# When the sums of a group of heads leave PSUM, and where the last group's sums lie: sigmoid attention before two gated MLPs

## Chip, core and metric

The kernel runs on one core of a Trainium2 chip. The metric is the device time of one execution in microseconds (us), as a median over runs; lower is better. The engines are named as the profile names them: PE multiplies matrices (PEld are its weight loads), ACT computes activations and copies, DVE does elementwise work and 32x32 transposes, SP issues nearly all DMAs. PE writes its results to PSUM, eight banks of 2 KB per partition, and ACT or DVE bring them from there to SBUF.

## What is computed

```python
# q, k, v: (4, 12, 448, 64), float32
scores = scale * np.matmul(q, k.transpose(0, 1, 3, 2)) - np.log(S)
attn = 1.0 / (1.0 + np.exp(-scores))
attn_out = np.matmul(attn, v)                 # 4 batches, 12 heads
x = attn_out.transpose(0, 2, 1, 3).reshape(4, 448, 768)
# then two gated MLPs in a row, each: h = act(x @ w_in); u, v = halves of h
# v normalized over its columns, then mixed over the sequence by w_spatial, plus b_spatial
# out = (u * mixed v) @ w_out        (the second adds its own x)
```

The attention is a sigmoid, not a softmax, so no row of scores has to be complete before its values can be summed.

## The kernel before

The attention works on groups of four heads, numbered n = 0 to 11 (three per batch, batches in the order 1, 0, 3, 2). The 448 keys are cut in chunks r = 0, 1, 2 of 128 keys and a rest r = 3 of 64. `scores` computes one chunk for the four heads of a group (24 matmuls, L500, each head in its own 32 rows of the array), `scores_rest` the rests of an even group and of the odd one behind it together (L518). Such a step is called a unit here; `weigh` puts two sigmoids on ACT behind it (L473, one per two heads, tiles a and ar).

`values` sums attention times v. An item (r, x) is the chunk r for the two heads of the pair x; a group has eight, and all go to one tile av of two banks: x = 0 in its first bank, x = 1 in its second. An item is two fp32 matmuls (L538), and the profile shows each of these as two records, so that four records are one item. When all four items of a pair are summed, `gather` copies the pair's bank to SBUF on ACT (L558): two copies (392 and 70 columns) in an odd batch, one of 448 in an even one.

Two consecutive groups, an even and an odd one, take 7 units, and 42 units in all are laid out in a fixed order. `units` and `sums` say which items follow which unit. PE and ACT run this order as it is written; nothing reorders it. The even group's last items are (3,0), (2,0), (2,1), all behind one unit, (3,0) bringing both pairs. The odd group's are (1,1), (2,0) behind one unit and (0,1), (2,1) behind the next; that next unit is the L518 one.

PSUM in the attention is four tiles of two banks, in a ring: a unit of scores takes two tiles from its head and gives them back once its sigmoids are issued, a group takes one for av with its first item and gives it back once it is gathered. So a unit, or a group's first item, waits until ACT has read what its tile held before. These waits are set by the framework from the tiles' uses; they are for a whole tile: an item that writes the second bank of av waits for a copy issued earlier out of the first.

Behind the last unit `done` puts six casts of the first MLP's input on ACT (L659) and six subtractions on DVE (L660). The last group's last four items come behind it in the program, then the first MLP, which opens with `hv` (L672, 18 matmuls of 512 columns into a tile t of the pool ps_t). The PSUM pools of the MLPs (ps_t, ps_av, ps_sc) are laid where the attention's pool ps_att was, and ps_t's first tile waits for what was in that pool at its place.

The lines that matter: L350 the ring, L352 `banks_of`, L526 to L548 `values` with `gather`'s calls, L558 the copies, L608 the warm-up that takes the ring's last tile, L933 and L943 to L945 the pools.

Of the kernel before, what the change touches and what calls it, by code (L numbers as in the profile page):

```python
# [9 lines left out]
F32 = mybir.dt.float32  # L10
# [16 lines left out]
def tile_sigmoid_attention_two_gated_mlps(  # L27
# [36 lines left out]
    P = 128  # L64
# [17 lines left out]
    xs = [const.tile([P, KF * ROW + PAD], F32, name=f"x{i}") for i in range(B // 2)]  # L82
# [256 lines left out]
    spatial.waiting = [load_w_sp(l1, j) for j in range(4)]  # L339


    def attention(apool, epool, ps_att, done):
        G = H // 4
        NG = B * G

# [1 line left out]
            b, i = divmod(n, G)  # L347
            return b ^ 1, i

        ring, open_sums = list(range(4)), {}  # L350

        def banks_of(k, name):  # L352
            return ps_att.tile([P, 2, 512], F32, tag=f"s{k}", name=name, bufs=1)
        raws, turned, ops, vs, att = {}, {}, {}, {}, {}

        def load_qk(n, xs="kq"):
# [109 lines left out]
        def score_banks():  # L466
            ks = [ring.pop(0) for _ in range(2)]
            return ks, [banks_of(k, "sc") for k in ks]
# [57 lines left out]
        def values(n, r, x):  # L526
            if n not in open_sums:
                k = ring.pop(0)
                open_sums[n] = k, banks_of(k, "av"), [0, 0]
            k, av, count = open_sums[n]  # L530
            vt, vr = vs[n]
            xs = (x,) if r < 3 else (0, 1)
            for x in xs:
                at = REST * ((x + n) % 2)
                ps = slice(at, at + REST)
                for o in range(2):
                    h = 2 * x + o
                    nc.tensor.matmul(  # L538
                        av[o * D:(o + 1) * D, x, :S],
                        vt[:, h, r] if r < 3 else vr[ps, o], att[n, r][:, h] if r < 3 else att[n, r][ps, h],  # L540
                        start=(count[x] == 0), stop=(count[x] == 3),
                    )
                count[x] += 1
            for x in xs:
                if count[x] == 4:
                    gather(n, x, av[:, x])
            if count == [4, 4]:
                ring.append(k)  # L548

        def gather(n, x, av):  # L550

            b, i = place(n)
            y = chunk_of(b, 2 * i + x)
            o = av[:, :S].rearrange("p (c t) -> p t c", c=TC)

            def back(at, t0, t1):
                dst = y[:, at:at + (t1 - t0) * TC]
                nc.scalar.copy(out=dst.rearrange("p (t c) -> p t c", c=TC), in_=o[:, t0:t1])  # L558

            if b % 2 == 0:  # L560
                back(0, 0, 32)
            else:
                t = 3 * P // TC
                back(SPAN, 0, t + 1)
                back(S - 3 * P % TC, t, 32)
# [34 lines left out]
        def weigh_up(s):  # L600
            for n, r, x in sums.get(s, ()):
                values(n, r, x)
# [3 lines left out]
        load_qk(1, "qk")  # L606
        later.pop("rows")()
        warm = banks_of(ring[-1], "av")[:, 0]  # L608
        for _ in range(9):
            nc.tensor.matmul(warm[:, :P], ident, ident, start=True, stop=True)  # L610
        turn(0)
        for s in range(U + 2):
# [3 lines left out]
            n = 2 * p + (1 if step < 2 else 2 if step < 6 else 3)  # L616
# [10 lines left out]
            if step in (0, 4):  # L627
                n = 2 * p + 2 + step // 4
# [8 lines left out]
            if s >= U:  # L637
                spatial.tick(1)

        return open_sums[NG - 1][0]  # L640


    class Mlp:
# [279 lines left out]
    with tc.manual_schedule():  # L923
# [4 lines left out]
        apool = tc.tile_pool(name="apool", bufs=1)  # L928
# [1 line left out]
        m1, m2 = Mlp(l1), Mlp(l2)  # L930

        psum = bass.MemoryType.PSUM
        ps_att = tc.tile_pool(name="ps_att", bufs=1, space=psum)  # L933

        def operands_made():
            apool.__exit__(None, None, None)
# [3 lines left out]
            m1.split_x(0, 0, KD)  # L940

        with tc.tile_pool(name="epool", bufs=1, side="right") as epool:
            last = attention(apool.__enter__(), epool, ps_att.__enter__(), operands_made)  # L943
        ps_att.__exit__(None, None, None)
        for x in ("ps_av", "ps_t", "ps_sc") if last == 0 else ("ps_t", "ps_av", "ps_sc"):  # L945
            later[x] = ctx.enter_context(tc.tile_pool(name=x, bufs=2, space=psum))

        later["opool"] = ctx.enter_context(tc.tile_pool(name="opool", bufs=1))
        with tc.tile_pool(name="fpool", bufs=1) as fpool:
# [47 lines left out]
            for b in range(B):  # L997
                last = b == B - 1
# [56 lines left out]
            for b in range(B):  # L1055
                last = b == B - 1
# [85 lines left out]
```

## Time and profile before

| | us |
|---|---|
| median of 3 runs | 562.26 (561.35 to 564.97) |
| profiled execution | 561.34 |
| its span on the core | 559.6 |
| PE busy in the span | 547.8 (98%) |
| ACT busy | 217.5 (39%) |
| DVE busy | 359.6 (64%) |

The span runs from the first to the last instruction that the profile shows; 1.74 us of the profiled execution lie around it. The attention takes about the first 144 us, the two MLPs the rest. A busy PE is one on which a matmul is in flight.

### The profile page before, as it was taken

To read this page: it belongs to the slowest core of one execution; us is meant where nothing else is said; L and a number is where in the kernel's file an instruction comes from. 1 tells how busy PE (TensorE), PEld (TensorE's weight loads), DVE (VectorE), ACT (ScalarE), POOL (GpSimd) and SP (SyncE) were. 2 spreads that over 40 slices of the span, in tenths; PEclk is the share of its full clock that TensorE was granted. 3 is DMA by queue.
4 is the path that set the end of the run, shared out by engine and by line. 5 is a ranking of instruction groups with operands and counts; after the bars stand their busy time and mean duration, and the time that the engine had idled before them with its cause. 6 is when DMAs were issued, how large, how long until landed. Compare 5 with 4: busy or idle time off the path is not lost.

```text
span 559.6 us, 9090 instructions
## 1 busy us (share of the span) xinstructions
PE 547.8 (98%) x3486; PEld 438.6 (78%) x3486; DVE 359.6 (64%) x749; ACT 217.5 (39%) x373; POOL 32.5 (6%) x62
## 2 busy tenths in 40 slices
PE   8999999999899999999999999999999999999997
PEld 5445444454589899898898889998999889989886
DVE  6999897882388789899764987851542173324311
ACT  6676666677234142353352146320311042103101
POOL 0000000000020100200200012000100020001000
PEclk9999999999999999999999999999999999999999
DMA  8878646341232165363336443200410032003003
GB/s 280 223 220 257 188 138 229 102 146 48 47 96 70 62 177 126 86 179 104 113 125 163 116 131 117 85 0 1 77 24 0 2 57 43 1 11 60 15 1 112
DMA packets 95531, 56.44 MB, mean 101 GB/s; under 512 B 67328, under 2 KB 83712, under 8 KB 95488
## 3 DMA queue, kind: packets, MB, share of 16 engines
q1 hardware_dynamic: 95344, 55.60, 36.5%
q8 instruction: 27, 0.44, 0.4%
q10 hardware_dynamic: 144, 0.26, 0.1%
q14 instruction: 16, 0.13, 0.1%
HBM read 44.83 MB, written 11.01 MB: 100 GB/s over the span
## 4 chain that ended last, share of the span: by engine, by line
PE 94%; ACT 4%; DMA 1%; DVE 0%; issue 0%; ACTq 0%
PE t L672 17%; PE t L718 17%; PE av L538 10%; PE sc L804 10%; PE sc L500 8%; PE t L738 6%; PE av L804 5%; PE av L738 3%; PE sc L738 3%; PE sc L814 3%; PE t L900 3%; PE av L900 3%; ACT a L473 3%; PE sc L518 2%; PE av L814 1%; PE t L814 1%
## 5 line engine op out<-in xcount | busy, mean ns | idle before, releaser
L473 ACT ACTIVATE a<-sc,small 128x896 f32<-128x896 f32 x72 | 67.3, 1007 | 29.6 <-PE sc L500 29.1
L538 PE MATMUL av<-a,vt 128*64 128x448 f32 x288 | 62.3, 552 | 6.4 <-ACT xe L558 3.5
L681 DVE BATCH_NORM_STATS2 st<-vr 128x6 f32<-128x512 f32 x28 | 19.4, 694 | 70.2 <-ACT vr L678 70.2
L678 ACT ACTIVATE vr<-t 128x512 f32<-128x512 f32 x28 | 16.7, 598 | 95.4 <-PE t L672 95.4
L500 PEld LDWEIGHTS sc<-opq,opk 32*128 32x128 f32 x840 | 39.8, 183 | 17.9 <-issue 12.7
L538 PEld LDWEIGHTS av<-a,vt 128*64 128x64 f32 x288 | 17.4, 136 | 44.6 <-issue 27.8
L500 PE MATMUL sc<-opq,opk 32*128 32x448 f32 x840 | 49.9, 373 | 0.0
L672 PE MATMUL t<-vh,xh 128*128 128x512 f32 x112 | 41.6, 392 | 0.6 <-ACT xe L558 0.6
L748 DVE SCALAR_TENSOR_TENSOR gt<-t,bb 128x448 f32<-128x448 f32 x16 | 10.9, 682 | 45.7 <-PE t L738 45.7
L683 POOL TENSOR_SCALAR st<-st 128x1 f32<-128x1 f32 x28 | 10.8, 384 | 472.1 <-DVE st L682 472.1
L672 PE MATMUL t<-vh,xl 128*128 128x512 f32 x98 | 38.2, 390 | 0.0
L756 ACT CAST gh<-u 128x448 fp32r<-128x448 f32 (+1 forms) x16 | 8.6, 540 | 71.8 <-DVE u L752 71.8
L718 PE MATMUL t<-xh,uh 128*128 128x448 f32 x96 | 34.8, 363 | 0.0
L718 PE MATMUL t<-xh,ul 128*128 128x448 f32 x96 | 34.8, 362 | 0.0
L718 PE MATMUL t<-xl,uh 128*128 128x448 f32 x96 | 34.6, 360 | 0.0
L738 PE MATMUL t<-sh,v 128*128 128x448 f32 x112 | 32.8, 362 | 0.0
L672 PE MATMUL t<-vl,xh 128*128 128x512 f32 x84 | 32.7, 389 | 0.0
L660 DVE TENSOR_TENSOR xl<-x,xh 128x512 fp32r<-128x512 f32 (+1 forms) x32 | 20.0, 654 | 19.1 <-ACT xh L659 19.1
L718 PE MATMUL t<-xh,vl 128*128 128x448 f32 x96 | 29.6, 362 | 0.0
L723 ACT ACTIVATE u<-t 128x448 f32<-128x448 f32 x32 | 17.4, 544 | 24.9 <-PE t L718 24.7
L700 ACT CAST v<-vr 128x512 fp32r<-128x512 f32 x24 | 14.9, 621 | 30.5 <-DVE vr L692 30.5
L672 PE MATMUL t<-m,xh 128*128 128x512 f32 x84 | 26.4, 395 | 0.0
(210 smaller groups left out, 1280.3 us busy)
## 6 DMA issues: line engine op xcount, KB each, us to landing
w<-in_moe_w_in_dram SPq DMA_DIRECT2D x24, 256.0 KB, 3.2
inq<-in_q_dram SPq DMA_DIRECT2D x12, 448.0 KB, 5.7
ink<-in_k_dram SPq DMA_DIRECT2D x11, 448.0 KB, 5.1
vt<-in_v_dram SPq DMA_DIRECT2D x48, 96.0 KB, 3.7
w<-in_moe_w_out_dram SPq DMA_DIRECT2D x18, 256.0 KB, 3.0
we<-in_moe_w_in_dram SPq DMA_DIRECT2D x6, 512.0 KB, 4.4
we<-in_moe_w_in_dram SPq DMA_DIRECT2D x8, 384.0 KB, 3.8
out_dram<-y SPq DMA_DIRECT2D x48, 56.0 KB, 1.9
```

Of the source, the lines that this page charges most:

```text
L473: nc.scalar.activation(a[:, dst], sc[x][..., :S], AF.Sigmoid, bias=bias_s, scale=scale)
L500: nc.tensor.matmul(banks[h][:, :S], opk[ps, x, o:o + P], opq[ps, y, S * j:S * (j + 1)], start=(t == 0), stop=(t == 5), tile_position=(32 * ...
L538: nc.tensor.matmul(av[o * D:(o + 1) * D, x, :S], vt[:, h, r] if r < 3 else vr[ps, o], att[n, r][:, h] if r < 3 else att[n, r][ps, h], star ...
L660: nc.vector.tensor_tensor(out=pair[1][:, :n], in0=src, in1=raw(pair[0][:, :n]), op=ALU.subtract)
L672: nc.tensor.matmul(ps[:, :FF], a, w, start=(c == 0 and n == 0), stop=(c == self.kc - 1 and n == 2),)
L681: nc.vector.bn_stats(out=st, in_=vr)
L718: nc.tensor.matmul(ps[:, :S], w, a, start=(c == 0 and n == 0), stop=(c == self.kc - 1 and n == 2),)
L723: nc.scalar.activation(u, ps[:, :S], AF.Relu if L.n == 1 else AF.Gelu_apprx_tanh)
L738: nc.tensor.matmul(ps[:, :S], a, w, start=(n == 0), stop=(n == len(todo) - 1))
L804: nc.tensor.matmul(self.o[m][:, :n_cols], w, a, start=(not second and i == 0 and n == 0), stop=(second and i == KF - 1 and n == 2),)
L814: nc.tensor.matmul(ps[:, :cols.stop - cols.start], a, w, start=(not second and i == 0 and n == 0), stop=(second and i == KF - 1 and n == 2),)
L900: nc.tensor.matmul(ps[:, :FF], x, w[:, c], start=(c == 0 and n == 0), stop=(c == KD - 1 and n == 2),)
```

## The change

`gather` is called for both pairs when the whole group is summed (`count == [4, 4]`), not for each pair when its own four items are. The rest item of an odd group takes its pairs in the order 1, 0. So it reads partitions 0 to 63 first and 64 to 127 behind them, as an even group's does. The ring starts as [0, 3, 1, 2], and tile 3 comes from a pool of its own, ps_last. It is the same ring with its tiles renamed, so that the last group's av is tile 3. ps_last is closed first, then ps_att, and the three pools of the MLPs come in one fixed order, which is also the one that the program took before.

```diff
@@ attention
-        ring, open_sums = list(range(4)), {}
+        ring, open_sums = [0, 3, 1, 2], {}
 
         def banks_of(k, name):
-            return ps_att.tile([P, 2, 512], F32, tag=f"s{k}", name=name, bufs=1)
+            pool = ps_att if k < 3 else ps_last
+            return pool.tile([P, 2, 512], F32, tag=f"s{k}", name=name, bufs=1)
@@ values
-            xs = (x,) if r < 3 else (0, 1)
+            xs = (x,) if r < 3 else (n % 2, 1 - n % 2)
...
                 count[x] += 1
-            for x in xs:
-                if count[x] == 4:
+            if count == [4, 4]:
+                for x in range(2):
                     gather(n, x, av[:, x])
-            if count == [4, 4]:
                 ring.append(k)
@@ the pools
-        ps_att = tc.tile_pool(name="ps_att", bufs=1, space=psum)
+        ps_att, ps_last = [tc.tile_pool(name=x, bufs=1, space=psum) for x in ("ps_att", "ps_last")]
...
+        ps_last.__exit__(None, None, None)
         ps_att.__exit__(None, None, None)
-        for x in ("ps_av", "ps_t", "ps_sc") if last == 0 else ("ps_t", "ps_av", "ps_sc"):
+        for x in ("ps_t", "ps_av", "ps_sc"):
             later[x] = ctx.enter_context(tc.tile_pool(name=x, bufs=2, space=psum))
```

Lines from L354 to L543 stand one lower in the changed kernel (L538 is L539 there, L473 is L474, L500 is L501); L558 and what follows stand where they stood.

On ACT, around the end of the first odd group (n = 1), the order before: six sigmoids of three units, the copies of pair 0 (392 and 70 columns), the sigmoids of the L518 unit, the copies of pair 1.

```order
L473 ACTIVATE a<-sc,small 128x896 x6
L558 COPY x_65<-av 128x392
L558 COPY x_65<-av 128x70
L473 ACTIVATE ar<-sc,small 128x896 x2
L558 COPY x_65<-av 128x392
L558 COPY x_65<-av 128x70
L473 ACTIVATE a<-sc,small 128x896 x6
```

The same place now:

```order
L474 ACTIVATE a<-sc,small 128x896 x6
L474 ACTIVATE ar<-sc,small 128x896 x2
L558 COPY x_65<-av 128x392
L558 COPY x_65<-av 128x70
L558 COPY x_65<-av 128x392
L558 COPY x_65<-av 128x70
L474 ACTIVATE a<-sc,small 128x896 x6
```

Pair 0's copies have moved behind the sigmoids of one more unit. Around an even group's end ACT's order is as it was; there the copies' waits change.

On PE, the end of the last group (n = 11) and the first matmuls of the MLP, with the engines that each row waits for in brackets (names with DMAHW are loads that have landed). Before, the eight matmuls of the last items (1,1), (2,0), (0,1), (2,1) and `hv`:

```order
L538 MATMUL av<-a,vt 64x448 [waits Activation_49]
L538 MATMUL av<-a,vt 64x448
L538 MATMUL av<-a,vt 64x448 [waits Activation_49]
L538 MATMUL av<-a,vt 64x448
L538 MATMUL av<-a,vt 64x448 [waits Activation_49]
L538 MATMUL av<-a,vt 64x448 x3
L672 MATMUL t<-vh_73,xh 128x512 [waits DMAHW3_49,DMAHW2_49,DMAHW4_49,DMAHW1_49,DMAHW5_49,DMAHW0_49,DMAHW6_49,DVE_49,Activation_49]
```

and now:

```order
L539 MATMUL av<-a,vt 64x448 [waits Activation_49]
L539 MATMUL av<-a,vt 64x448
L539 MATMUL av<-a,vt 64x448 [waits Activation_49]
L539 MATMUL av<-a,vt 64x448 x3
L539 MATMUL av<-a,vt 64x448 [waits Activation_49]
L539 MATMUL av<-a,vt 64x448
L672 MATMUL t<-vh_73,xh 128x512 [waits DMAHW3_49,DMAHW2_49,DMAHW4_49,DMAHW1_49,DMAHW5_49,DMAHW0_49,DMAHW6_49,PE_49,Activation_49]
```

The fifth matmul, the first of item (0,1), no longer waits for ACT. The seventh now waits for the sigmoid of its own second pair of heads, which a wait on the later copy covered before. `hv` still waits for ACT, but for another instruction there: by the semaphore values of the two programs it was the second gather copy, and it is the first L659 cast now.

## Rows read from the trace of the kernel before

**Rows 1.** Stages: window and its us, then busy us of each engine (instructions), PE clock, DMA
```profile
5.53:144.53 139.00, 131.93 (x1448) 64.56 (x1449) 115.76 (x220) 94.81 (x129) 0.00 (x0) 1.00 0.60 179
144.53:540.00 395.47, 395.47 (x1927) 356.06 (x1928) 240.43 (x520) 118.45 (x237) 31.81 (x56) 1.00 0.29 73
```

**Rows 2.** Waits of PE: who waited for whom, us in total, times, longest
```profile
PE av L538 <- ACT xe L558: 3.5, 3, 2.0
PE av L538 <- ACT x L558: 2.8, 4, 0.7
```

**Rows 3.** Timeline of PE, groups 0 and 1: start, us, instructions, [idle before and releaser]
```profile
17.05 0.98 PE L538 MATMUL av<-ar,vr 64*64 64x448 f32 x8
17.97 0.97 PE L538 MATMUL av<-a,vt 128*64 128x448 f32 x4
19.64 0.97 PE L538 MATMUL av<-a,vt 128*64 128x448 f32 x4 [0.70 <-ACT x L558]
20.55 2.70 PE L500 MATMUL sc<-opq,opk 32*128 32x448 f32 x48
23.20 1.08 PE L538 MATMUL av<-ar,vr 64*64 64x448 f32 x8
24.21 1.72 PE L538 MATMUL av<-a,vt 128*64 128x448 f32 x8
25.86 1.50 PE L500 MATMUL sc<-opq,opk 32*128 32x448 f32 x24
...
30.64 1.72 PE L538 MATMUL av<-a,vt 128*64 128x448 f32 x8
32.29 2.74 PE L500 MATMUL sc<-opq,opk 32*128 32x448 f32 x48
```

**Rows 4.** Timeline of ACT in the same stretch
```profile
17.08 1.90 ACT L473 ACTIVATE a<-sc,small 128x896 f32<-128x896 f32 x2 [0.59 <-PE sc L500]
18.99 0.60 ACT L558 COPY x<-av 128x392 f32<-128x392 f32 x2
...
30.81 1.91 ACT L473 ACTIVATE ar<-sc,small 128x896 f32<-128x896 f32 x2 [0.95 <-PE sc L518]
32.60 0.60 ACT L558 COPY x<-av 128x392 f32<-128x392 f32 x2
33.89 3.71 ACT L473 ACTIVATE a<-sc,small 128x896 f32<-128x896 f32 x4 [0.68 <-PE sc L500]
```

**Rows 5.** Timeline of PE, groups 9 to 11 and the first MLP's start
```profile
122.60 2.74 PE L500 MATMUL sc<-opq,opk 32*128 32x448 f32 x48
...
130.76 0.97 PE L538 MATMUL av<-a,vt 128*64 128x448 f32 x4
132.40 0.97 PE L538 MATMUL av<-a,vt 128*64 128x448 f32 x4 [0.66 <-ACT x L558]
133.30 2.71 PE L500 MATMUL sc<-opq,opk 32*128 32x448 f32 x48
...
136.97 3.23 PE L538 MATMUL av<-a,vt 128*64 128x448 f32 x16
142.17 1.72 PE L538 MATMUL av<-a,vt 128*64 128x448 f32 x8 [1.98 <-ACT xe L558]
144.53 0.50 PE L672 MATMUL t<-vh,xh 128*128 128x512 f32 x1 [0.63 <-ACT xe L558]
```

**Rows 6.** Timeline of ACT in that stretch
```profile
122.88 0.54 ACT L558 COPY x<-av 128x448 f32<-128x448 f32 x1
...
138.47 2.19 ACT L659 CAST xh<-x 128x512 fp32r<-128x512 f32 x4
...
141.57 0.55 ACT L558 COPY xe<-av 128x448 f32<-128x448 f32 x1
```

**Rows 7.** Groups of the page: weight loads of the scores (busy us, mean ns | idle)
```profile
L500 PEld LDWEIGHTS sc<-opq,opk 32*128 32x128 f32 x840 | 39.8, 183 | 17.9 <-issue 12.7
```

**Rows 8.** Timeline of DVE: operands of group 2, subtractions for the first MLP
```profile
22.04 1.08 DVE L456 TENSOR_TENSOR opq<-tq,opq 128x896 fp32r<-128x896 f32 x1
...
139.13 2.50 DVE L660 TENSOR_TENSOR xl<-x,xh 128x512 fp32r<-128x512 f32 x4 [10.42 <-ACT xh L659]
```

More of the change, by code (lines that the diff above doesn't have):

```diff
@@ L339, in tile_sigmoid_attention_two_gated_mlps, with attention @@
     spatial.waiting = [load_w_sp(l1, j) for j in range(4)]
-    def attention(apool, epool, ps_att, done):
+    def attention(apool, epool, ps_att, ps_last, done):
         G = H // 4
@@ L638, in attention @@
                 spatial.tick(1)
-        return open_sums[NG - 1][0]
+        assert open_sums[NG - 1][0] == 3
     class Mlp:
@@ L942, in tile_sigmoid_attention_two_gated_mlps @@
         with tc.tile_pool(name="epool", bufs=1, side="right") as epool:
-            last = attention(apool.__enter__(), epool, ps_att.__enter__(), operands_made)
+            attention(apool.__enter__(), epool, ps_att.__enter__(), ps_last.__enter__(), operands_made)
+        ps_last.__exit__(None, None, None)
         ps_att.__exit__(None, None, None)
-        for x in ("ps_av", "ps_t", "ps_sc") if last == 0 else ("ps_t", "ps_av", "ps_sc"):
+        for x in ("ps_t", "ps_av", "ps_sc"):
             later[x] = ctx.enter_context(tc.tile_pool(name=x, bufs=2, space=psum))
```

## The prediction

> **What bounds the kernel now.** I read the stages first [rows 1]. From 144.53 to 540 us PE is busy in all of 395.47 us: the MLPs wait for nothing, and whatever the attention gives back there moves the end by as much. In the attention, 5.53 to 144.53 us, PE is busy 131.93 of 139.00 us, so 7.1 us is idle; ACT works 94.81 us and DVE 115.76 us of it. PE's clock is the full one (1.00) in both stretches. So the question is what PE's 7 us are. The table of waits answers it [rows 2]: 3.5 + 2.8 = 6.3 us in seven waits of the value matmuls (L538) for a gather copy (L558).
>
> The timelines show how. In group 0 PE starts item (2,0) at 17.97 and has done its four records by 18.94. Then (2,1) stands until 19.64 [rows 3]. ACT started that unit's two sigmoids at 17.08, copied pair 0 from 18.99 for 0.60, and PE goes on 0.05 us behind the copy's end [rows 4]. The item writes the other bank of the tile; it waits because its tile is being read. Group 10 shows the same with 0.66 us [rows 5]; there are six such waits, one in each even group, and as the long one of rows 2 belongs to the last group, they hold 6.3 - 1.98 = 4.3 us. The last group is odd and pays otherwise: its pair 0 is copied behind the six casts of the first MLP's input, at 141.57 [rows 6], so its last two items stand 1.98 us, and `hv` then 0.63 us for the second copy [rows 5]. Odd groups before it do not stall: their pair 0 was copied a unit earlier.
>
> **What the change removes.** In an even group no copy is issued any more before (2,1). The price of one stall is more than its idle time, as weight loads and the filling of the array show again behind it: from the start of (2,0) to the next unit it is 20.55 - 17.97 = 2.58 us, where an unbroken run of the same eight records takes 32.29 - 30.64 = 1.65 [rows 3]. That is 0.93; in group 10 it is 133.30 - 130.76 - 1.65 = 0.89 [rows 5]. Six groups at 0.91: **5.5 us**.
>
> In the last group all items run in one piece. The sixteen records from 136.97 take 3.23 - 0.07 = 3.16 to the next start (0.07 is how far 1.72 stands over 1.65), eight more 1.65, so `hv` could start at 141.78 in place of 144.53: **2.75 us** [rows 5]. Its inputs are there: the first cast is done about 139.0 (138.47 and a quarter of 2.19), its subtraction starts at 139.13 and goes at some 0.63 us a piece [rows 6, 8], faster than `hv` uses them. Its tile t needs the attention's sigmoids out of the way, and those end where the casts begin. So the copies of the last group, now issued behind the casts and free of `hv`, cover themselves behind its matmuls. The pool of its own is what keeps them from `hv`; it costs nothing.
>
> **What it adds.** A group's tile is empty later, and a unit takes it two units on, with its second pair of heads. Queued behind the copies on ACT are the next unit's sigmoids; in the odd case they start at 33.89 [rows 4], and four copies started at 32.60 end at 33.71 (two blocks of 0.60, 0.1 overlapped as sigmoids on ACT are: 1.90 for two of 1.0). So ACT's next work is not late. The tile is, by little:
> - odd group, two-piece copies: ready 33.71; the unit that wants it starts half of 2.65 behind 32.29, at 33.62 [rows 3, 4]. With 0.05 for the hand-over PE is late by 0.14; if the weight load (0.18 [rows 7]) can't run ahead while it waits, by 0.32.
> - odd group, one-piece copies: 122.88 + 0.54 + 0.44 = 123.86, the unit at 122.60 + 1.33 = 123.93 [rows 5, 6]: 0, or 0.16 with the load.
> - even group: its copies now wait for (2,1), which ends at 17.97 + 1.72 = 19.69; ready 19.74 + 1.10 = 20.84, the unit at 19.62 + 1.33 = 20.95: 0, or 0.12; with one-piece copies 0.
>
> There are two odd groups of the first kind and three of the second (the last has no unit behind it), four even ones of the third kind and two that pay nothing. The low end is 2 x 0.14 = 0.3 us, the high end 2 x 0.32 + 3 x 0.16 + 4 x 0.12 = 1.6. I take **1.0**, half way: loads do overlap matmuls in an unbroken run, but no row shows what a load does that has to wait.
>
> The Trainium skill speaks against the change here: "PSUM — Partial Sum Buffer", section "Summary: rules for kernel authors", says to evacuate promptly, as PSUM is tight, and this change evacuates half of each group's sums later. By it the first rival below is what to expect. The same table tells to read PSUM in a different bank while a matmul runs, which the order before did; the 0.70 us are the program's wait and not a collision's price.
>
> **What I cost at nothing.** The swap of the pairs in an odd group's rest: its eight records take 24.21 - 23.20 = 1.01 us where an even group's take 17.97 - 17.05 = 0.92 [rows 3]. If the order is the reason, it gives 6 x 0.09 = 0.5 us; if the reason is the wait for a free tile in front of it, nothing. I take nothing and keep 0.5 for the low end. The ring's renaming changes no wait. DVE: group 2's operands are ready at 23.12 and used at 25.86 [rows 8, 3]; 2.7 us of room, where PE comes 0.9 earlier by then. That cover is the thinnest that I found; gone, it costs what the attention gained.
>
> **Sum.** 5.5 + 2.75 - 1.0 = 7.25 us. From the profiled execution, 561.34 (span 559.6 and 1.74 around it), this gives 554.1; that execution is 0.9 below the median of the three and equal to the lowest of them, so on the median it is 555.0. I predict **554.6**, between the two.
>
> **Rivals.**
> 1. *Held tiles cost what the early copies saved in part.* For it: the odd group's copies reach their unit with less than nothing to spare (33.71 against 33.62), and in eleven groups a small delay of ACT, such as an instruction that starts 0.3 us late, would go straight to PE. Against it: ACT is idle 0.6 to 2 us between its blocks. At the high end of above and 0.2 us more in each of eleven groups, 1.6 + 2.2 = 3.8: 8.25 - 3.8 = 4.45 us won, about 557.3. It decides when a group pays over 0.25 us on average.
> 2. *Another engine sets the attention's pace.* DVE works almost without a break through the first third; if operands and not PE set the pace, the 5.5 us fall away and only the end's 2.75 stay: about 559. Against it stands the room of 2.7 us, and that no wait of PE for DVE is in the table.
> 3. *The pool of its own does not free `hv`.* If t's first tile still waited for the last group's copies, these would run from 141.83, behind the items, for 0.55 + 0.44, and `hv` would start at 142.87: 1.1 us of the 2.75 lost, about 555.7. Against it: by the built program `hv` waits on ACT for the first cast.
> 4. *Slower.* One mechanism: the four copies come to stand in the way of the next sigmoids, and the next group's first items, which wait for these, start late in every pair of groups. From rows 4, ACT has 33.89 - 33.71 = 0.18 us to spare there. Slower than before it becomes when the eleven groups pay over 8.25 / 11 = 0.75 us each; at 1.3 us, two copies' length, it would be 561.3 + 6 = 567.
>
> **How the numbers follow.** The forecast's own case, 553.0 to 556.6, holds 0.74, with rival 3 in it. Rival 1, 556.6 to 559: 0.16. Rival 2: 0.07, up to no change at all. Rival 4: 0.03. The low end is 8.25 with no new wait and 0.5 from the swap, from 561.34: 552.6; I set 553.0. The high end takes in most of rival 1: 557.8. A measurement of this kernel can tell about 1%, 5.6 us, from no change, which from 562.26 is 556.6: the forecast's case lies below it, rivals 1 and 2 (0.16 + 0.07) above, within 1%. So faster 0.74, same 0.23, slower 0.03. The nearness of that bound is the main doubt: at the high end of the new waits 6.65 us are left.
>
> **What the profile after would show.** Right: no wait of L539 for a copy in the table; in group 0 eight value records in one run from about 17.97 to 19.69, the next unit at 19.62 in place of 20.55; four copies (two in an even batch) in one block of 1.0 to 1.1 us on ACT; `hv` without a wait, at about 137.3 (144.53 - 7.25); the second stage's 395 us unchanged; span near 552.3. New, small waits of L501 for L558, at most 0.3 us each, in the unit two behind a group's end. Wrong: L501 waits for L558 of over 0.4 us each (rival 1), L501 waits for DVE (rival 2), an idle PE in the MLPs, where the gain would be lost again, or sigmoids idle behind copies (rival 4).

## The result and the profile after

| | before | after |
|---|---|---|
| median | 561.42 us (6 runs, 561.28 to 564.97) | 553.94 us (6 runs, 553.67 to 554.35) |
| profiled execution | 561.34 us | 553.95 us |
| its span | 559.6 us | 552.2 us |
| PE busy in the span | 547.8 us | 547.5 us |
| first matmul of `hv` | 144.53 us | 137.14 us |
| from there to the end | 415.0 us | 415.0 us |

The medians lie 7.5 us apart, 1.3%. The ratio over all runs is 0.9855, 95% interval 0.9832 to 0.9879; the long execution of before (564.97 us) counts in it. The two profiled executions differ by 7.39 us, and all of it lies ahead of `hv`.

The stages after, with the same columns as [rows 1] (PE, PEld, DVE, ACT and POOL busy, PE clock, DMA share and GB/s), cut 0.09 us ahead of `hv`'s first matmul:

```profile
5.53:137.05 131.52, 131.39 (x1449) 65.61 (x1448) 114.28 (x218) 93.72 (x127) 0.00 (x0) 1.00 0.64 188
137.05:533.00 395.95, 395.95 (x1932) 356.42 (x1931) 241.72 (x523) 119.41 (x240) 31.79 (x56) 1.00 0.29 73
```

PE's work in the attention is nearly what it was (131.39 us busy, before 131.93), in 7.5 us less; its idle time there went from 7.1 us to 0.1. The second stage is one unbroken run of PE, as before. The table of PE's waits, five rows long before, holds one, the wait of the warm-up matmuls for their operand, which was there before too:

```profile
PE av L610 <- POOL ident masks.py:199: 1.3, 1, 1.3
```

PE's timeline of groups 0 and 1 (start, us, instructions, idle before), which answers to [rows 3]:

```profile
17.52 0.98 PE L539 MATMUL av<-ar,vr 64*64 64x448 f32 x8
18.43 1.72 PE L539 MATMUL av<-a,vt 128*64 128x448 f32 x8
20.09 2.77 PE L501 MATMUL sc<-opq,opk 32*128 32x448 f32 x48
22.79 1.04 PE L539 MATMUL av<-ar,vr 64*64 64x448 f32 x8
23.75 1.72 PE L539 MATMUL av<-a,vt 128*64 128x448 f32 x8
...
30.18 1.72 PE L539 MATMUL av<-a,vt 128*64 128x448 f32 x8
31.83 2.97 PE L501 MATMUL sc<-opq,opk 32*128 32x448 f32 x48
34.73 3.23 PE L539 MATMUL av<-a,vt 128*64 128x448 f32 x16
```

Items (2,0) and (2,1) are one run of eight records, and the next unit starts 1.66 us behind its start; it was 2.58. The price stands in the last rows: the two units behind the odd group take 34.73 - 31.83 = 2.90 us. Before, they took 34.96 - 32.29 = 2.67, with 32.29 from [rows 3] and the end from the row behind it:

```profile
34.96 3.23 PE L538 MATMUL av<-a,vt 128*64 128x448 f32 x16
```

ACT in that stretch, for [rows 4]:

```profile
17.54 1.91 ACT L474 ACTIVATE a<-sc,small 128x896 f32<-128x896 f32 x2 [0.60 <-PE sc L501]
20.20 1.12 ACT L558 COPY x<-av 128x392 f32<-128x392 f32 x4 [0.76 <-PE av L539]
...
30.35 1.91 ACT L474 ACTIVATE ar<-sc,small 128x896 f32<-128x896 f32 x2 [1.44 <-PE sc L519]
32.14 1.11 ACT L558 COPY x<-av 128x392 f32<-128x392 f32 x4
33.44 3.70 ACT L474 ACTIVATE a<-sc,small 128x896 f32<-128x896 f32 x4 [0.18 <-PE sc L501]
```

The four copies are one block. The second block ends at 33.25, and the unit that takes the tile was due at 31.83 + 1.33 = 33.16. The end of the attention, for [rows 5]:

```profile
132.48 4.73 PE L539 MATMUL av<-a,vt 128*64 128x448 f32 x24
137.14 0.50 PE L672 MATMUL t<-vh,xh 128*128 128x512 f32 x1
```

The last group's 24 records run in one piece and `hv` follows without a wait; from 136.97 to `hv` it took 7.56 us before, from 132.48 it takes 4.66.

### The profile page after: what moved, and what is told of

Same layout as the page of the kernel before. It is cut to its first block, busy times and chain, and to the rows that moved or that the text cites. A ratio compares the mean times of both kernels' runs of the same rounds, so it can differ in the third digit from the quotient of the medians.

```text
span 552.2 us, 9096 instructions
## 1 busy us (share of the span) xinstructions
PE 547.5 (99%) x3486; PEld 439.7 (80%) x3486; DVE 359.4 (65%) x749; ACT 217.4 (39%) x373; POOL 32.5 (6%) x62
## 4 chain that ended last, share of the span: by engine, by line
PE 99%; ACT 0%; issue 0%; POOL 0%; DVE 0%; POOLq 0%
PE t L672 17%; PE t L718 17%; PE av L539 13%; PE sc L804 10%; PE sc L501 9%; PE t L738 6%; PE av L804 5%; PE av L738 3%; PE sc L738 3%; PE sc L814 3%; PE t L900 3%; PE av L900 3%; PE sc L519 2%; PE av L814 2%; PE t L814 2%; PE av L610 1%
## 5 line engine op out<-in xcount | busy, mean ns | idle before, releaser
L474 ACT ACTIVATE a<-sc,small 128x896 f32<-128x896 f32 x72 | 67.3, 1007 | 25.0 <-PE sc L501 24.4
L539 PE MATMUL av<-a,vt 128*64 128x448 f32 x288 | 60.7, 550 | 0.1
L501 PEld LDWEIGHTS sc<-opq,opk 32*128 32x128 f32 x840 | 40.3, 183 | 18.2 <-issue 9.2
L501 PE MATMUL sc<-opq,opk 32*128 32x448 f32 x840 | 50.7, 375 | 0.0
L539 PEld LDWEIGHTS av<-a,vt 128*64 128x64 f32 x288 | 18.0, 136 | 36.1 <-issue 29.4
```

What stands on the lines that cost most here:

```text
L474: nc.scalar.activation(a[:, dst], sc[x][..., :S], AF.Sigmoid, bias=bias_s, scale=scale)
L501: nc.tensor.matmul(banks[h][:, :S], opk[ps, x, o:o + P], opq[ps, y, S * j:S * (j + 1)], start=(t == 0), stop=(t == 5), tile_position=(32 * ...
L539: nc.tensor.matmul(av[o * D:(o + 1) * D, x, :S], vt[:, h, r] if r < 3 else vr[ps, o], att[n, r][:, h] if r < 3 else att[n, r][ps, h], star ...
```

## Experiments

Theory: the time came from two places, six stalls of about 0.9 us in even groups and 2.9 us at the attention's end, and tiles that are held longer took back 0.8 us of it. Rivals: the pool does nothing, the swap of the pairs does something, held tiles cost nothing, or a large part of the gain is lost to operands.

### The copies alone

`gather` for both pairs behind the last item; one pool, the ring and the order as before.

```diff
-            for x in xs:
-                if count[x] == 4:
+            if count == [4, 4]:
+                for x in range(2):
                     gather(n, x, av[:, x])
-            if count == [4, 4]:
                 ring.append(k)
```

> The copies of both pairs behind the group's last item, as in the change; one pool for all four tiles, the ring and the order of pairs as before. My account: the six even stalls are gone (5.5 us), the last group's items run in one piece (about 2.9 us with what follows), the held tiles cost 0.8 us, and the first matmul of hv now waits for both copies of the last group, which start when its last item ends: 0.97 + 0.1 us of waiting. Sum 6.5 us under before, about 554.9 us, and 1.0 us above the changed kernel, with a wait of L671 for L557 of about 1 us. Rival (the pool of its own does nothing, since hv is held by its casts or subtractions anyway): no more than 0.2 us above the changed kernel, about 554.0 us.

Measured: 554.94 us, ratio to before 0.9865 (0.9839 to 0.9891), 1.0 us above the changed kernel, as expected. PE's timeline at the end shows where it is:

```profile
132.90 4.73 PE L538 MATMUL av<-a,vt 128*64 128x448 f32 x24
138.69 0.50 PE L671 MATMUL t<-vh,xh 128*128 128x512 f32 x1 [1.07 <-ACT xe L557]
```

The items run in one piece here too, but `hv` then stands 1.07 us for the last group's copies. So the pool of its own is worth 1.0 us once the copies are late, and `hv`'s own inputs don't hold it.

### The pool alone

Ring, pools and their order as in the change; copies pair by pair and the pairs' order as before.

```diff
-            if count == [4, 4]:
-                for x in range(2):
+            for x in xs:
+                if count[x] == 4:
                     gather(n, x, av[:, x])
+            if count == [4, 4]:
                 ring.append(k)
```

(This diff is against the changed kernel, as are those below unless they say otherwise; the pairs' order is taken back too.)

> The last group's tile in a pool of its own and the ring renamed; copies pair by pair and the order of pairs as before. My account: only the wait of hv for the second copy goes, 0.63 us and some 0.1 us of restart: 0.7 us under before, about 560.7 us; the seven waits of the value matmuls stay at 6.3 us. Rival (hv is held by its inputs): the time of before, 561.4 us. Rival (the ring's renaming moves banks and with them something else): another time than either by more than 0.5 us.

Measured: 561.46 us, ratio 0.9977 (0.9955 to 0.9998). Of its ten executions, those with a mean PE clock of 0.999 or more took 560.85 to 561.48 us; those of before, measured beside them, with such a clock 561.52 to 562.39. The medians of these, 560.97 and 561.85, lie 0.9 us apart, where 0.7 was expected. In the profiled execution the seven waits of the value matmuls are there (6.2 us) and `hv`'s is not:

```profile
PE av L539 <- ACT xe L559: 3.5, 3, 2.0
PE av L539 <- ACT x L559: 2.7, 4, 0.7
```

Its last eight value records, though, took 2.62 us in place of 1.72, and this execution was 562.85 us. That led to the last two experiments.

```profile
142.74 2.62 PE L539 MATMUL av<-a,vt 128*64 128x448 f32 x8 [1.98 <-ACT xe L559]
```

### Without the swap of the pairs

```diff
-            xs = (x,) if r < 3 else (n % 2, 1 - n % 2)
+            xs = (x,) if r < 3 else (0, 1)
```

> The changed kernel, but an odd group's rest item takes its pairs in the order 0, 1 again. My account: the order is worth nothing; the 0.09 us by which an odd group's rest takes longer than an even group's come from the wait for the sigmoids that free its tile. 553.9 us, within 0.2 us of the changed kernel, and the eight records of an odd group's rest take 0.95 to 1.01 us in both. Rival (the order matters): 6 x 0.09 = 0.5 us more, about 554.5 us, and these eight records go back to 1.01 us in each group.

Measured: 554.0 us (553.72 to 554.24), ratio 0.9846 (0.9823 to 0.9869). The changed kernel's time; the odd groups' eight rest records take 0.96 to 1.01 us here and 0.95 to 1.01 in the changed kernel, as in this timeline, 24.01 - 23.05 = 0.96:

```profile
23.05 1.03 PE L539 MATMUL av<-ar,vr 64*64 64x448 f32 x8
24.01 1.72 PE L539 MATMUL av<-a,vt 128*64 128x448 f32 x8
```

The order is worth nothing that can be seen. Before, the rests of the six odd groups took 6.02 us together; with the changed kernel it is 5.87, and 5.86 with the order taken back. Two experiments further down settle what this 0.15 us goes with. Even groups alone, with the order of before, has 5.82; the last group alone, with the changed order and the even groups' early copies, has 6.04. So it goes with the even groups' copies and not with the order. That it comes from the sigmoids that free the tile, as I had expected, no run shows by itself.

### Odd groups copy early again

```diff
-            if count == [4, 4]:
-                for x in range(2):
+            early = n % 2 == 1 and n < NG - 1
+            for x in xs:
+                if count[x] == 4 and early:
                     gather(n, x, av[:, x])
+            if count == [4, 4]:
+                if not early:
+                    for x in range(2):
+                        gather(n, x, av[:, x])
                 ring.append(k)
```

> The changed kernel, but the five odd groups before the last copy pair 0 as soon as it is summed, a unit earlier, as before the change. My account: the late copies of the odd groups are what costs the changed kernel 0.23, 0.09, 0.23 and 0.05 us in the second unit behind a group's end (four of the five; in the fifth the next wait hides it): 0.6 us less, about 553.35 us, with these pairs of units back at 2.66 to 2.67 us and no stall of the items, since pair 0's copy is done by then. Rival (the longer units have another cause): the changed kernel's time, 553.95 us. Rival (an early copy stalls the odd group's last items as it does the even group's): 5 x 0.9 us more, about 558.4 us.

Measured: 553.09 us (552.85 to 553.87), ratio 0.9834 (0.9811 to 0.9858). This is the best version, 0.9 us under the kernel without the swap, which was measured beside it on the same chip. PE and ACT behind group 1:

```profile
29.70 1.72 PE L539 MATMUL av<-a,vt 128*64 128x448 f32 x8
31.35 2.73 PE L501 MATMUL sc<-opq,opk 32*128 32x448 f32 x48
34.01 2.48 PE L539 MATMUL av<-a,vt 128*64 128x448 f32 x12
```

```profile
28.31 0.61 ACT L563 COPY x<-av 128x392 f32<-128x392 f32 x2
29.87 1.91 ACT L474 ACTIVATE ar<-sc,small 128x896 f32<-128x896 f32 x2 [0.95 <-PE sc L519]
31.66 0.60 ACT L563 COPY x<-av 128x392 f32<-128x392 f32 x2
```

The pair of units takes 34.01 - 31.35 = 2.66 us again. Pair 0 is copied at 28.31, behind the sigmoids of the unit before, in time that ACT had idle, and is done by 28.92, before the odd group's last items at 29.70; so nothing stalls. Over the five odd groups the units take 0.59 us less than in the changed kernel; the other 0.3 us lie within the spread of the two kernels' runs.

### Odd groups copy everything twice

```diff
             if count == [4, 4]:
-                for x in range(2):
-                    gather(n, x, av[:, x])
+                for _ in range(2 if n % 2 == 1 and n < NG - 1 else 1):
+                    for x in range(2):
+                        gather(n, x, av[:, x])
                 ring.append(k)
```

> The changed kernel, but the five odd groups before the last copy both pairs twice (the same values to the same place), so that their tile is held about 1.0 us longer and ACT's next sigmoids stand 1.0 us further back. My account: there is no room left, so each microsecond goes to PE: the second unit behind such a group waits 1.0 us more, five times: about 4.5 to 5.5 us above the changed kernel, 558.4 to 559.5 us. Rival (ACT's idle 0.2 to 2.4 us between its blocks takes it): under 1 us above the changed kernel.

Measured: 558.37 us, ratio 0.9908 (0.9877 to 0.9939): 4.4 us above the changed kernel, the low end of what was expected. PE and ACT behind group 1:

```profile
32.27 1.70 PE L501 MATMUL sc<-opq,opk 32*128 32x448 f32 x26
34.76 1.50 PE L501 MATMUL sc<-opq,opk 32*128 32x448 f32 x22 [0.79 <-ACT x L559]
```

```profile
32.58 2.13 ACT L559 COPY x<-av 128x392 f32<-128x392 f32 x8
34.51 3.79 ACT L474 ACTIVATE a<-sc,small 128x896 f32<-128x896 f32 x4
```

The second unit starts its first two heads and then stands until the eight copies are done at 34.71. From the timelines of the five groups, the two units take 0.66 to 1.02 us more each, 4.4 us in all. ACT's idle time elsewhere helps nothing: the tile is wanted at one moment.

### Even groups alone

Against the kernel before: both pairs together where n is even, all else as it was.

```diff
             for x in xs:
-                if count[x] == 4:
+                if count[x] == 4 and n % 2:
                     gather(n, x, av[:, x])
             if count == [4, 4]:
+                if n % 2 == 0:
+                    for x in range(2):
+                        gather(n, x, av[:, x])
                 ring.append(k)
```

> The kernel before, with the copies of both pairs behind the last item in the six even groups alone; odd groups, the last one too, the pool and the order of pairs as before. My account: six stalls of 0.92 us go, held tiles give back 0.2 us: 5.3 us under before, about 556.1 us, and the last group's waits of 1.98 and 0.63 us stay. Rival (PE's gain in the attention is given back because operands from DVE come late): less than 3 us under before.

Measured: 556.57 us (556.01 to 559.04), ratio 0.9887 (0.9854 to 0.9921). The profiled execution, 556.01 us, is 5.3 us under the profiled one of before: the six stalls, less what the held tiles take. The three executions at full clock have a median of 556.51, also 5.3 us under the 561.80 of before measured beside them. The end is untouched:

```profile
136.82 1.72 PE L538 MATMUL av<-a,vt 128*64 128x448 f32 x8 [1.98 <-ACT xe L561]
139.17 0.50 PE L675 MATMUL t<-vh,xh 128*128 128x512 f32 x1 [0.63 <-ACT xe L561]
```

### The last group alone, and all but the last group

A pattern had shown by now: some kernels' times spread over 2 to 4 us, others' over about 1 at most, and each long execution had a mean PE clock under 0.998. Two kernels part the short stalls from the long one. `together` decides whether a group copies both pairs behind its last item: for the last group alone (`n == NG - 1`) in the first, for all the others (`n < NG - 1`) in the second.

```diff
-            if count == [4, 4]:
-                for x in range(2):
+            together = n == NG - 1
+            for x in xs:
+                if count[x] == 4 and not together:
                     gather(n, x, av[:, x])
+            if count == [4, 4]:
+                if together:
+                    for x in range(2):
+                        gather(n, x, av[:, x])
                 ring.append(k)
```

> The changed kernel, but only the last group copies both pairs together; groups 0 to 10 copy each pair as soon as it is summed, as before the change. My account: the six stalls of 0.7 us idle are back and the held tiles free, so 5.5 - 0.8 = 4.7 us above the changed kernel, about 558.6 us. On the clock: the runs of before split by their mean granted clock, 1.000 to 0.999 (561.3 to 562.4 us) and 0.997 to 0.994 (562.9 to 565.2 us). If what drops the clock is the long wait at the attention's end, all runs here have 0.999 or more and lie within 0.8 us. Rival (the six short stalls drop it): some of the runs have 0.997 or less and are 1.4 to 3.7 us longer.

> The changed kernel, but the last group copies pair 0 as soon as it is summed, behind the six casts, as before the change; its pool is its own, so hv does not wait for the second copy. My account: the wait of 1.98 us idle comes back, the rest of the change stays: 2.1 to 2.3 us above the changed kernel, about 556.2 us in executions with a clock of 0.999 or more. On the clock: if the long wait is what drops it, some of the runs (of before it was about half) have a mean clock of 0.997 or less and are 1.4 us or more longer than the others. Rival (the six short stalls drop it): all runs have 0.999 or more.

Measured: the first 558.83 us (558.40 to 559.28), ratio 0.9922 (0.9897 to 0.9948), the second 557.31 us (556.56 to 558.37), ratio 0.9895 (0.9866 to 0.9924). The first, with all six short stalls and no long one, has a mean clock of 0.999 or 1.000 in six of six executions, which lie within 0.88 us (0.8 expected). The second, with the long stall alone, is under 0.998 in four of six. Its two executions at full clock took 556.56 and 556.88, 0.4 to 0.7 us more than I had expected; why is not shown. The four others took 557.25 to 558.37, 0.4 to 1.8 us more than these two. I had expected 1.4 or more, so the clock fell as the long-wait account says, but its price was put too high. In its profiled execution (558.22 us) the stages behind the stall (window, its us, PE, PEld, DVE, ACT, POOL busy, PE clock, DMA) read:

```profile
138.09:138.33 0.24, 0.24 (x2) 0.20 (x4) 0.24 (x2) 0.00 (x0) 0.00 (x0) 1.00 0.58 84
138.33:141.74 3.41, 3.41 (x10) 1.06 (x7) 0.41 (x1) 0.53 (x1) 0.00 (x0) 0.50 0.14 25
141.74:150.00 8.26, 8.26 (x38) 6.83 (x37) 2.02 (x5) 0.73 (x2) 0.79 (x2) 1.00 0.08 12
```

and PE's timeline there:

```profile
132.88 3.23 PE L539 MATMUL av<-a,vt 128*64 128x448 f32 x16
138.09 3.06 PE L539 MATMUL av<-a,vt 128*64 128x448 f32 x8 [1.98 <-ACT xe L563]
141.08 0.80 PE L677 MATMUL t<-vh,xh 128*128 128x512 f32 x1
```

PE stands for 1.98 us and starts again at 138.09. Then, 0.24 us later, the granted clock falls to the lower of its two levels, 1.2 GHz of 2.4, for 3.41 us. The eight records take 3.06 us where they take 1.72 at the full clock. The profile of the pool alone, where PE starts again at 142.74, has the same fall 0.69 us behind the restart:

```profile
142.74:143.43 0.69, 0.69 (x4) 0.34 (x6) 0.66 (x2) 0.00 (x0) 0.00 (x0) 1.00 0.62 98
143.43:146.84 3.41, 3.41 (x10) 1.51 (x7) 0.00 (x0) 0.53 (x1) 0.00 (x0) 0.50 0.12 20
```

## Why the prediction was right

Its range, 553.0 to 557.8 us, and its value, 554.6, held the median of 553.94. By its own steps:

- **Six stalls, 5.5 us.** Measured from the start of (2,0) to the next unit in all six even groups: 5.51 us. The kernel with the even groups alone won 5.3 with the held tiles in it. That the price is more than the idle 4.3 us, with the restart in it, was right.
- **The end, 2.75 us.** 7.56 - 4.66 = 2.90. The two parts were told apart: without the pool `hv` waits 1.07 us again, and the pool alone, with early copies, gives 0.9 by the medians at full clock (0.7 expected). The last group alone, with the six short stalls, is 2.8 us under before by the medians at full clock (558.83 against 561.64).
- **New waits, 1.0 us between 0.3 and 1.6.** Measured on the pairs of units: 0.23, 0, 0.09, 0.23 and 0.05 us in the odd groups, 0.17 in all even ones, 0.76 together. The sizes lie between a wait without its weight load (0.14 and 0) and one with it (0.32 and 0.16). The zero is the one behind group 3, where ACT starts its next block 0.3 us late in both kernels, so that the two units take 2.97 us with or without the held tile. That the odd groups pay this was shown by taking it away (2.66 us again) and by doubling the copies (0.66 to 1.02 us more per group). For the even groups the last group alone shows it: there they copy early, and their six pairs of units take 15.96 us together, before 15.97 and in the changed kernel 16.14. The waits of L501 for L558 that the forecast named as a sign do not stand in PE's table; PEld's has two, 0.3 us in all.
- **The swap, nothing.** Nothing.
- **The sum, 7.25.** 5.51 + 2.90 - 0.76 = 7.65, and 0.1 from odd groups' rests that wait a little less. `hv` came 7.39 earlier. The 0.4 between are in the first units: the first L519 unit took 2.22 us, 0.46 more than in the execution of before, and PE's weight loads show 0.4 us of wait for a transpose of DVE (L418) there. This unit took 1.69 to 2.70 us in the other kernels' executions too, and the three longest (2.64 to 2.70) show 0.8 us of such a wait; it is the start that varies. So it is in part luck that the sum lies within 0.14 us of the measured 7.39: the forecast's steps were 0.4 us too low together, and the slower start of this execution took as much away.
- **No loss behind the attention.** 415.0 us from `hv` to the end in both.

The value of 554.6 lay 0.7 us high because I set it between the profiled execution and the median of three. The median of six is 561.42: the profiled execution had been the typical one, and one of the three (564.97) an execution of another kind, as the last two experiments suggest. Of the rivals, the first (held tiles) is a true mechanism of this kernel with a small price: 0.8 us, not 3.8. The Trainium skill's rule to evacuate promptly ("PSUM — Partial Sum Buffer", "Summary: rules for kernel authors") holds as far as this price goes: following it in the odd groups alone wins 0.6 to 0.9 us more, and following it in the even ones costs 5.5. The second rival (operands) did not show: with PE up to 7 us earlier no wait for DVE appears in PE's table, and the 0.4 us in PEld's lies in the first units, ahead of every group's end. The fourth would need held tiles of over 0.75 us in each of eleven groups; they reach such a price only where the copies are doubled, 0.66 to 1.02 us in each of five.

## What to carry to other kernels

A copy out of a finished half of a tile stalls the matmuls into its other half when waits are kept per tile; ask which of the two is wanted first. Copy early where ACT is idle and no matmul into the same tile comes behind the copy soon, and late where the last items follow at once; a rule for all groups gives one of the two away. And what stands ahead of the copy in ACT's queue sets the price of a stall, not the copy alone: 0.6 us of copy cost 0.9 us behind two sigmoids and, by the timeline at full clock, about 2.2 us behind six casts (the 2.90 at the end less some 0.7 for `hv`'s own wait; 1.98 of it idle).

## What was not expected of the hardware

A long wait of PE can cost twice. Of 33 executions of before that were measured beside the experiments, 18 had a mean granted clock under 0.998, and these took 562.88 to 565.2 us; the other 15 took 561.42 to 562.5. All four kernels with the 1.98 us wait at the attention's end show it in part of their runs (before 18 of 33, the pool alone 4 of 10, even groups alone 1 of 4, all but the last group 4 of 6). None of the kernels without it does: 0 of 30 (the changed one 0 of 6, copies alone 0 of 4, no swap 0 of 5, odd groups early 0 of 5, copies twice 0 of 4, last group alone 0 of 6), though they have waits of up to 1.3 us at the start and 1.07 us between attention and MLP. All but the last group differs from the changed kernel only in the copy that causes this wait, and has the low clock in 4 of 6 against 0 of 6; so the fall goes with the long wait. Two profiles, of the pool alone and of all but the last group, show the place: the lower clock is granted for 3.41 us, beginning 0.69 and 0.24 us behind PE's restart after the 1.98 us. Half the clock for 3.41 of some 560 us takes 0.003 off the mean, so a mean of 0.997 is one such stretch; those of 0.994 would by this estimate be two, which no profile here shows. What decides in which executions the clock falls stays open. The medians give the change 7.5 us; that its time no longer spreads by over 3 us is a gain which neither profiled execution shows, as both ran at the full clock.
